# Attention block: four small moves around the key-tile loop, and the copy of the sums from ScalarE to VectorE

## Chip, cores, metric

One core of a Trainium2 chip. The metric is device time of one launch in microseconds; lower is better.

## The reference

```python
# x: 1 x 2048 x 640, H = 32 heads of Dh = 20
qkv = (layernorm(x) @ wqkv) -> q, k, v            # each 32 heads x 2048 x 20
p = softmax(einsum("bhqd,bhkd->bhqk", q, k) * 20 ** -0.5)
h = x + merge_heads(einsum("bhqk,bhkd->bhqd", p, v)) @ wo
out = h + (silu(layernorm(h) @ w_gate) * (layernorm(h) @ w_up)) @ w_down   # F = 1728
```

All tensors are float32.

## The kernel before

The program has three stages: the projections to q, k and v with layer norm (until about 320 us), the attention (until about 1445 us), and the feed-forward network. The change lies in the attention.

**Units.** Heads go in 8 groups of `G` = 4, queries in `NC` = 4 chunks of 512. A group g and a chunk c make a unit, u = 4 g + c, so there are `NU` = 32 units. Within a unit a loop runs over `NT` = 16 key tiles of 128 keys (`kt`). The instructions of each engine stand in the order in which Python writes them; nothing reorders them.

**One key tile.** The string `ORDER` = "WhSmsSHMs" gives the sequence of one key tile: W is the weighted sum of the values with the exponentials of two tiles ago (`weigh`, L1338, into the bank `acc`); S and s are the four score products (`scores`, L1328), each followed on ScalarE by an exponential (L1334, `probs`); h, H, m and M are products for later units' maxima (L272), whose results VectorE reduces (L292, L307) into `mx`. So a tile gives ScalarE four exponentials and VectorE three reductions. Each kind of product takes its banks in turn (`ps_one` four, `ps_max` three).

**Maxima.** Softmax needs each query's largest score before its exponentials. They are computed ahead, for the next one to two units. When a unit v has all of them (`full`), `max_all` reduces and negates them (L315, `neg`). They then go as extra rows into `queries[v]`, whose four rows the score products of unit v wait for:

- For units with c < 3, `max_parts` splits them on GpSimd, `max_turn` turns them on VectorE (L331) and stores them to DRAM (`m_d`, L332), and `max_load` loads them back (L342, four DMAs). The dictionary `later` says in which key tile each of these is issued, right behind W.
- For units with c = 3 (and unit 1), `max_finish` turns them on TensorE (L347), splits them on ScalarE and VectorE (L89, L90, `m`) and writes the rows with four DMAs (L354).

**End of a unit.** The last W of a unit runs in the second tile of the next unit's loop; right behind it `row_sums` copies `acc` to `o` (L1348) and sends the row sums to `r` (L1351, four DMAs). Later tiles of the same loop run `reciprocals` (L1359 on VectorE, its store L1361), `spread` (L1367, `rb`), a product on GpSimd (L1373), and the stores of the outputs (`store_o`, L1376, four DMAs to `o_d`).

**SyncE's queue.** All these DMAs, the loads of keys, values and queries for later units (L176, L193) and the stores and loads of weights that GpSimd prepares for the feed-forward network in between (`preparing`, L1137, L1166) go through SyncE's one queue in program order: one that waits holds those behind it.

Of the kernel before, what the change touches and what calls it, by code (L numbers as in the profile page):

```python
# [13 lines left out]
AF = mybir.ActivationFunctionType  # L14
# [16 lines left out]
NG = H // G  # L31
# [13 lines left out]
def tile_block(ctx: ExitStack, tc: tile.TileContext, x, wqkv, wo, wg, wu, wd, out):  # L45
    nc = tc.nc
# [41 lines left out]
    def split(src, hi, lo, lo_engine=nc.vector):  # L88
        nc.scalar.activation(hi, src, AF.Copy)  # L89
        lo_engine.tensor_tensor(out=lo, in0=src, in1=hi.bitcast(F32), op=ALU.subtract)  # L90
# [221 lines left out]
    def max_all(u):  # L312

        ends[u] = stk.tile([P, G * TPC], F32, name="neg", tag="neg", bufs=2)
        nc.vector.tensor_reduce(  # L315
            ends[u], mxs[u].rearrange("p b h t k -> p (b h t) k"), axis=AX.X, op=ALU.max, negate=True
        )
# [10 lines left out]
    def max_turn(u):  # L328

        turned = stk.tile([P, 2 * G * TPC], F32, name="turned", bufs=2)  # L330
        nc.vector.transpose(turned, ends.pop(u).bitcast(F32).rearrange("p i n -> p (i n)"))  # L331
        nc.sync.dma_start(m_d[u % 2], turned)  # L332

    def max_load(u):

        n = 2 * TPC
        rows = m_d[u % 2].rearrange("(q i r) c -> i r q c", q=4, i=2)
        for b in range(2):
            for i in range(2):
                row = b * ROW + NPART + i  # L340
                dst = queries[u][row : row + 1].bitcast(F32).rearrange("r j c -> r (j c)")
                nc.sync.dma_start(dst, rows[i, b * n : (b + 1) * n])  # L342

    def max_finish(u):

        m = (ps_one if u else ps_max)()[: G * TPC, :P]
        nc.tensor.transpose(m, ends.pop(u), ident)  # L347
        parts = stk.tile([G * TPC, 2, P], F32R, name="m2", tag="m2", bufs=1)
        split(m, parts[:, 0], parts[:, 1], nc.vector)
        for b in range(2):  # L350
            for i in range(2):
                row = b * ROW + NPART + i
                first = b * 2 * TPC
                nc.sync.dma_start(  # L354
                    queries[u][row : row + 1].bitcast(F32).rearrange(
                        "r j (t p) -> r (j t) p", t=TPC
                    ),
                    parts[first : first + 2 * TPC, i, :].bitcast(F32),
                )
# [963 lines left out]
    def scores(u, kt, j, probs):  # L1323

        p, b = divmod(j, 2)
        rows = slice(b * ROW, b * ROW + NPART + 2)
        ps = ps_one()
        nc.tensor.matmul(  # L1328
            ps,
            keys[u // NC][rows, p, kt * P : (kt + 1) * P],  # L1330
            queries[u][rows, p, :],
            start=True, stop=True,
        )
        nc.scalar.activation(probs[p][:, b, :], ps, AF.Exp, scale=scale)  # L1334
# [10 lines left out]

    def row_sums(acc, *queues):
        o = pc.tile([P, CH], F32, name="o", bufs=2)
        nc.scalar.activation(o, acc, AF.Copy)  # L1348
        r = pc.tile([P, 16], F32, name="r")
        for j in range(G):  # L1350
            queues[j % len(queues)].dma_start(  # L1351
                r[32 * j : 32 * j + 32, :],
                o[32 * j + DH : 32 * j + DH + 1, :].rearrange("r (p f) -> r p f", p=32),
            )
        return o, r
# [24 lines left out]
    todo, tail, accs, later, full, now = [], [], {}, {}, [], [0]  # L1380
    left = {u: sum(2 for a in rest if a[0] == u) for u in range(1, NU)}

    whole, halves_of = [], []

    def counted(u, n):
        left[u] -= n
# [3 lines left out]
    def next_max(b):  # L1390
        if not whole and rest:
            a = rest.pop(0)
            whole.extend((*a, i) for i in (b, 1 - b))
        if whole:
            a = whole.pop(0)
            max_one(*a)
            counted(a[0], 1)

    def next_half(b):

        if not halves_of and rest:
            a = rest.pop(0)
            halves_of.extend((i, a, []) for i in range(2))
        if not halves_of:
            return
        i, a, banks = halves_of[0]
        if not banks:
            banks.append(ps_max())
            max_half(banks[0], i, *a, b)
        else:  # L1410
            nc.tensor.keepalive_nop([nc.tensor.lower_ap(banks[0])])
            max_half(banks[0], i, *a, b)
            max_halves(banks[0], i, *a)
            counted(a[0], 2 * i)
            halves_of.pop(0)
# [11 lines left out]
    preparing = prepare_weights()  # L1427
# [3 lines left out]
    for u in range(NU):  # L1431
        g, c = divmod(u, NC)
        if g == NG - 1 and c >= 2:
            _, first, ln, flips, _ = ahead
            extra = [*first, *ln, lambda: None, *flips]
        for kt in range(NT):
            now[0] = u * NT + kt
            probs = [pp.tile([P, 2, CH], F32, name="probs") for _ in range(2)]
            heads = [[0, 2], [1, 3]]
            for op in ORDER if rest or whole or halves_of else LAST_ORDER:  # L1440
                if op in "mM":
                    next_max(int(op == "M"))
                elif op in "hH":
                    next_half(int(op == "H"))
                elif op in "sS":
                    scores(u, kt, heads[op == "S"].pop(0), probs)
                else:
                    if len(todo) == 2:
                        weigh_next()
                    for f in later.pop(now[0], ()):  # L1450
                        f()
                    if extra:
                        extra.pop(0)()
                    if preparing and u and kt not in (3, 4):
                        preparing.pop(0)()
                    if now[0] == (NU - NC) * NT + 8:
                        unit_ring, last_ring = weight_rings()
                        unit_ring.fill()
                        last_ring.fill()
            todo.append((u, kt, probs))  # L1460
            for v in full:
                max_all(v)
                if v % NC == NC - 1 or v == 1:
                    later.setdefault(now[0] + 2, []).append(lambda v=v: max_finish(v))
                else:
                    max_parts(v)
                    later.setdefault(now[0] + 4, []).append(lambda v=v: max_turn(v))
                    later.setdefault(now[0] + 6, []).append(lambda v=v: max_load(v))
            full.clear()
            if kt == 6 and u + 3 < NU:  # L1470
                load_queries(u + 3)
            if kt == 10 and u == 0:
                fill_ones(k_stk[1])
            if kt >= 8 and kt % 2 == 0 and c == 1 and g + 1 < NG:
                load_keys(g + 1, slice((kt - 8) // 2 * CH, (kt - 6) // 2 * CH))
            if kt >= 8 and kt % 2 == 0 and c == 2 and g + 1 < NG:
                load_values(g + 1, (kt - 8) // 2 * TPC, (kt - 6) // 2 * TPC)

            sooner = u >= NU - 2
            if kt == (3 if sooner else 4) and tail:  # L1480
                reciprocals(u - 1, tail[0][2], nc.sync)
                rb = spread(u - 1, nc.sync)
            if kt == (6 if sooner else 9) and tail:
                store_o(u - 1, tail[0][1], rb, nc.gpsimd, None)
            if kt == (7 if sooner else 11) and tail:
                store_o(u - 1, tail.pop()[1], rb, None, nc.sync)
            if g == NG - 1 and c >= 1:
                at = 8 if sooner else NT - 4
                if kt == at:
                    ahead = projection(  # L1490
                        c - 1, ps_max if c < NC - 1 else (lambda: ps_b())
                    )
                if kt in (at, at + 1, 12 if sooner else 14):
                    ahead[0][min(kt - at, 2)]()
                    if kt == at + 1 and c < NC - 1:
                        ahead[4]()
            k = 2 * (u - NU + 8)
            if kt in (12, 13) and 0 <= k + kt - 12 < ND:
                if k + kt == 12:
                    assert not preparing  # L1500
                    wo_hi = pc.tile([P, ND, D], F32R, name="wo_hi", bufs=1)
                    wo_lo = pc.tile([P, ND, D], F32R, name="wo_lo", bufs=1)
                load_wo(k + kt - 12)
            if kt in (2, 3) and 0 <= k + kt - 4 < ND:
                split_wo(k + kt - 4)
# [4 lines left out]
    u, o, r = tail.pop()  # L1510
# [561 lines left out]
```

## Time and profile before

| | us |
|---|---|
| median of 3 runs (lowest, highest) | 2011.97 (2009.52, 2014.36) |
| the profiled execution, and its span | 2012.87, 2010.4 |
| busy: TensorE, weight loads | 1985.1, 1268.7 |
| busy: VectorE, ScalarE, GpSimd | 1599.5, 1440.1, 789.4 |
| exponentials (L1334, 2048) | 1056.1 |
| reductions of maxima (L292 980, L307 492) | 671.8, 335.8 |

The granted TensorE clock was 0.999. A row of the timeline gives the start from the span's beginning, the duration, the engine, the line, the operation and the tile written and read; in brackets the engine's idle time ahead of it and what ended it. "q" behind an engine marks its queue (SPq: SyncE issuing a DMA). A row of the waits gives the waiter, who ended the wait, the total, the number and the longest.

### The profile page before, as it was taken

What the parts mean: (1) busy time and instruction counts of PE and PEld (TensorE: products, weight loads), DVE (VectorE), ACT (ScalarE), POOL (GpSimd) and SP (SyncE); (2) the same over time, 40 slices, a digit from 0 to 9 for tenths busy, and PEclk for the clock granted to TensorE, in tenths of its full rate; (3) what the DMA queues carried; (4) which work ended last, traced back from release to release, by engine and by line L of the source; (5) the groups of instructions that cost most, each with busy time, mean ns of one, the idle gap of its engine ahead of it and who ended that gap; (6) DMA issues with size and microseconds to landing.
All of it is one profiled execution on the core that took longest, in us unless ns stands there. A gap on an engine that the chain in (4) does not pass through costs nothing. (4 is left out here: it accounts for less than half of the span.)

```text
span 2010.4 us, 41923 instructions
## 1 busy us (share of the span) xinstructions
PE 1985.1 (99%) x14794; PEld 1268.7 (63%) x14794; DVE 1599.5 (80%) x2831; ACT 1440.1 (72%) x2827; POOL 789.4 (39%) x1182
## 2 busy tenths in 40 slices
PE   8999999999999999999999999999999999999998
PEld 6999995444444444444444444455598888888887
DVE  5687778899999899998999999975477666676667
ACT  4678778999999999999999999987633222212221
POOL 7464424343453443443400011011155544844465
PEclk9999999999999999999999999999999999999999
DMA  7887563443634544435412132222268655974642
GB/s 244 255 258 257 183 206 78 128 140 105 193 103 141 152 135 138 157 127 175 150 60 68 40 86 58 79 63 62 62 215 278 228 168 174 359 248 160 203 146 93
DMA packets 199350, 310.48 MB, mean 154 GB/s; under 512 B 53744, under 2 KB 87856, under 8 KB 198120
## 3 DMA queue, kind: packets, MB, share of 16 engines
q1 hardware_dynamic: 192552, 284.21, 44.0%
q0 software_dynamic: 6496, 23.60, 4.0%
q8 instruction: 120, 1.97, 0.4%
q14 instruction: 86, 0.70, 0.1%
q10 hardware_dynamic: 96, 0.00, 0.0%
HBM read 208.11 MB, written 99.19 MB: 153 GB/s over the span
## 5 line engine op out<-in xcount | busy, mean ns | idle before, releaser
L1334 ACT ACTIVATE probs<-ps_one 128x512 f32<-128x512 f32 x2048 | 1056.1, 612 | 46.7 <-PE ps_one L1328 37.2
L292 DVE TENSOR_REDUCE mx<-ps_max 128x1 f32<-128x512 f32 x980 | 671.8, 686 | 90.6 <-PE ps_max L272 88.0
L272 PEld LDWEIGHTS ps_max<-k_stk,q_stk 60*128 60x128 f32 x1964 | 294.2, 185 | 462.8 <-DVE mx L307 393.5
L1328 PE MATMUL ps_one<-q_stk,k_stk 62*128 62x512 f32 x2048 | 570.4, 427 | 2.7 <-DMA q_stk<-m 1.8
L272 PE MATMUL ps_max<-k_stk,q_stk 60*128 60x256 f32 (+1 forms) x1964 | 565.5, 376 | 2.5 <-DVE mx L292 1.2
L1338 PE MATMUL acc<-probs,v_stk 128*32 128x512 f32 x4096 | 546.1, 605 | 0.1
L307 DVE TENSOR_REDUCE mx<-ps_max 128x2 f32<-128x512 f32 x492 | 335.8, 683 | 0.4 <-PE ps_max L272 0.4
L1328 PEld LDWEIGHTS ps_one<-q_stk,k_stk 62*128 62x128 f32 x2048 | 304.9, 184 | 15.0 <-ACT probs L1334 11.3
L1750 DVE TENSOR_TENSOR tmp<-ps_a,tmp 128x512 f32<-128x512 f32 x208 | 141.3, 690 | 122.2 <-PE ps_a L1535 96.6
L262 DVE TENSOR_REDUCE mx<-ps_max 128x2 f32<-128x512 f32 x288 | 180.8, 685 | 63.7 <-PE ps_max L240 60.2
L252 ACT ACTIVATE ps_max<-ps_max 128x512 f32<-128x512 f32 x288 | 151.6, 583 | 42.9 <-PE ps_max L240 40.3
L1629 PE MATMUL ps_b<-halves,yp 128*128 128x320 f32 x1032 | 179.0, 308 | 1.5 <-DMA halves<-j_d 1.3
L1629 PEld LDWEIGHTS ps_b<-halves,yp 128*128 128x128 f32 x1032 | 165.2, 188 | 17.5 <-POOL yp L90 1.5
L1535 PE MATMUL ps_a<-t,units 128*128 128x512 f32 x624 | 162.5, 396 | 0.0
L1338 PEld LDWEIGHTS acc<-probs,v_stk 128*32 128x32 f32 x4096 | 80.7, 108 | 128.1 <-issue 119.9
L90 POOL TENSOR_TENSOR yp<-y,yp 128x256 fp32r<-128x256 f32 x96 | 60.2, 628 | 189.7 <-ACT yp L89 189.7
L1535 PE MATMUL ps_a<-z,units 128*128 128x512 f32 x516 | 133.8, 394 | 0.0
L1535 PEld LDWEIGHTS ps_a<-t,units 128*128 128x128 f32 x624 | 112.6, 188 | 18.5
L1373 POOL TENSOR_TENSOR o<-o,rb 128x512 f32<-128x512 f32 x31 | 39.8, 1284 | 194.2 <-DMA rb<-r_d 60.6
L1634 DVE TENSOR_TENSOR h<-ps_b,h 128x320 f32<-128x320 f32 x248 | 110.1, 482 | 6.8 <-PE ps_b L1629 5.4
L671 PE MATMUL ps_one<-z_hi,w_lo 64*128 64x512 f32 x380 | 113.4, 392 | 0.0
L671 PE MATMUL ps_one<-z_lo,w_hi 64*128 64x512 f32 x380 | 112.1, 392 | 0.0
(228 smaller groups left out, 2746.5 us busy)
## 6 DMA issues: line engine op xcount, KB each, us to landing
units<-w_d SPq DMA_DIRECT2D x186, 256.0 KB
w_d<-stage SPq DMA_DIRECT2D x106, 256.0 KB
halves<-j_d SPq DMA_DIRECT2D x70, 320.0 KB
j_d<-stage SPq DMA_DIRECT2D x42, 320.0 KB
k_stk<-k_d SPq DMA_DIRECT2D x64, 160.0 KB
q_stk<-q_d SPq DMA_DIRECT2D x64, 160.0 KB
raw<-k_d SPq DMA_DIRECT2D x62, 160.0 KB
raw<-q_d SPq DMA_DIRECT2D x54, 160.0 KB
```

What stands on the lines that cost most here:

```text
L252: nc.scalar.activation(ps, ps, AF.Relu)
L262: nc.vector.tensor_reduce(mx[:, b, :, t, kc], ps.rearrange("p (j n) -> p j n", j=2), axis=AX.X, op=ALU.max,)
L272: nc.tensor.matmul(ps, queries[u][rows, pair, t * P : (t + 1) * P], keys[u // NC][rows, pair, k0:k1], start=True, stop=True, skip_group_ch ...
L292: nc.vector.tensor_reduce(mx[:, b, pair, t, kc : kc + 1], ps, axis=AX.X, op=ALU.max)
L307: nc.vector.tensor_reduce(max_slots(u)[:, :, pair, t, slot], ps.rearrange("p (j n) -> p j n", j=2), axis=AX.X, op=ALU.max,)
L671: nc.tensor.matmul(ps, a[rows], b[rows], start=(i == n == 0), stop=(i == 1 and n == last), skip_group_check=True,)
L1328: nc.tensor.matmul(ps, keys[u // NC][rows, p, kt * P : (kt + 1) * P], queries[u][rows, p, :], start=True, stop=True,)
L1334: nc.scalar.activation(probs[p][:, b, :], ps, AF.Exp, scale=scale)
L1338: nc.tensor.matmul(acc[32 * j : 32 * j + 32, :], values[u // NC][:, kt, j * VW : j * VW + 32], probs[j // 2][:, j % 2, :], start=(kt == 0) ...
L1535: nc.tensor.matmul(ps.rearrange("p (t n) -> p t n", t=TPC), w[k][:, i], z[k][:, :, j], start=(first and m == 0), stop=(last and m == len(n ...
L1629: nc.tensor.matmul(ps, a, b, start=(n == 0), stop=(n == len(pairs) - 1))
L1750: add = lambda out, ps, x: nc.vector.tensor_tensor(out=out, in0=ps, in1=x, op=ALU.add)
```

## The change

1. `row_sums` copies `acc` on VectorE instead of ScalarE.
2. `max_turn` and `max_load` are issued 3 and 5 key tiles after `full` instead of 4 and 6. `max_finish` is issued at the end of the next tile's sequence instead of behind the W of the tile after that, through the new list `behind_step`; in a tile where that list holds something, no step of `preparing` is taken.
3. The keys of the next group are loaded in the first unit of a group instead of the second (except in group 0).
4. The reciprocals come at tile 5 instead of 4, except in the last two units.
5. In units with c = 2 (except unit 30) the four output stores come at tile 13 instead of 11.

```diff
     def row_sums(acc, *queues):
         o = pc.tile([P, CH], F32, name="o", bufs=2)
-        nc.scalar.activation(o, acc, AF.Copy)
+        nc.vector.tensor_copy(o, acc)
...
-                    if preparing and u and kt not in (3, 4):
+                    if preparing and u and kt not in (3, 4) and not behind_step:
                         preparing.pop(0)()
...
             todo.append((u, kt, probs))
+            while behind_step:
+                behind_step.pop(0)()
             for v in full:
                 max_all(v)
                 if v % NC == NC - 1 or v == 1:
-                    later.setdefault(now[0] + 2, []).append(lambda v=v: max_finish(v))
+                    behind_step.append(lambda v=v: max_finish(v))
                 else:
                     max_parts(v)
-                    later.setdefault(now[0] + 4, []).append(lambda v=v: max_turn(v))
-                    later.setdefault(now[0] + 6, []).append(lambda v=v: max_load(v))
+                    later.setdefault(now[0] + 3, []).append(lambda v=v: max_turn(v))
+                    later.setdefault(now[0] + 5, []).append(lambda v=v: max_load(v))
...
-            if kt >= 8 and kt % 2 == 0 and c == 1 and g + 1 < NG:
+            if kt >= 8 and kt % 2 == 0 and c == (0 if g else 1) and g + 1 < NG:
                 load_keys(g + 1, slice((kt - 8) // 2 * CH, (kt - 6) // 2 * CH))
...
-            if kt == (3 if sooner else 4) and tail:
+            if kt == (3 if sooner else 5) and tail:
                 reciprocals(u - 1, tail[0][2], nc.sync)
                 rb = spread(u - 1, nc.sync)
             if kt == (6 if sooner else 9) and tail:
                 store_o(u - 1, tail[0][1], rb, nc.gpsimd, None)
-            if kt == (7 if sooner else 11) and tail:
+            if kt == (7 if sooner else 13 if c == 2 else 11) and tail:
                 store_o(u - 1, tail.pop()[1], rb, None, nc.sync)
```

VectorE's order at the start of unit 11, after the change. `mx_134` holds maxima of a later unit; L292 and L307 are the three reductions of a key tile.

```order
L292 TENSOR_REDUCE mx_134<-ps_max 128x1 x2
L307 TENSOR_REDUCE mx_134<-ps_max 128x2
L292 TENSOR_REDUCE mx_134<-ps_max 128x1
L1348 COPY o<-acc 128x512
L292 TENSOR_REDUCE mx_134<-ps_max 128x1
L307 TENSOR_REDUCE mx_134<-ps_max 128x2
L292 TENSOR_REDUCE mx_134<-ps_max 128x1 x2
```

Before, nothing stood between these two L292; the copy is new on this engine, between the last reduction of one tile and the first of the next.

VectorE's order some key tiles later in unit 11, before the change:

```order
L307 TENSOR_REDUCE mx_134<-ps_max 128x2
L292 TENSOR_REDUCE mx_134<-ps_max 128x1
L1359 RECIPROCAL r<-r 128x16
L292 TENSOR_REDUCE mx_135<-ps_max 128x1
L307 TENSOR_REDUCE mx_134<-ps_max 128x2
L292 TENSOR_REDUCE mx_135<-ps_max 128x1
L315 TENSOR_REDUCE neg<-mx_134 128x16
L292 TENSOR_REDUCE mx_135<-ps_max 128x1
```

and after it:

```order
L292 TENSOR_REDUCE mx_134<-ps_max 128x1
L292 TENSOR_REDUCE mx_135<-ps_max 128x1
L307 TENSOR_REDUCE mx_134<-ps_max 128x2
L292 TENSOR_REDUCE mx_135<-ps_max 128x1
L315 TENSOR_REDUCE neg<-mx_134 128x16
L1359 RECIPROCAL r<-r 128x16
L292 TENSOR_REDUCE mx_135<-ps_max 128x1
```

The reciprocal has moved one tile on and now stands directly behind L315.

SyncE's queue in the second half of unit 10 (c = 2), before the change. `v_stk` are values for the next group, `w_d` prepared weights, `q_stk<-m` the four rows of maxima for unit 11.

```order
L193 DMA v_stk_5606<-v_d 128x4x96 x2
L1376 DMA o_d<-o 20x512 x4
L1137 DMA w_d_86<-stage 128x512
L193 DMA v_stk_5606<-v_d 128x4x96
L354 DMA q_stk<-m_11431 1x8x128 x4
```

and after it:

```order
L193 DMA v_stk_5606<-v_d 128x4x96 x2
L354 DMA q_stk<-m_11412 1x8x128 x4
L193 DMA v_stk_5606<-v_d 128x4x96
L1376 DMA o_d<-o 20x512 x4
L193 DMA v_stk_5606<-v_d 128x4x96
```

The rows of maxima have passed the output stores, one value load and the weight store; the output stores now come behind them.

More of the change, by code (lines that the diff above doesn't have):

```diff
@@ L1381, in tile_block @@
     left = {u: sum(2 for a in rest if a[0] == u) for u in range(1, NU)}
-    whole, halves_of = [], []
+    whole, halves_of, behind_step = [], [], []
     def counted(u, n):
```

## The prediction

> **What bounds the kernel now.** I read the page first, then the windows of the attention, the waits of ScalarE and VectorE in it, and last the timeline around the starts of units. The page alone misleads:
>
> ```profile
> PE 1985.1 (99%) x14794; PEld 1268.7 (63%) x14794; DVE 1599.5 (80%) x2831; ACT 1440.1 (72%) x2827; POOL 789.4 (39%) x1182
> POOL 7464424343453443443400011011155544844465
> ```
> ```profile
> 500.00:600.00 100.00, 100.00 (x766) 42.54 (x765) 91.70 (x157) 99.43 (x195) 45.74 (x85) 1.00 0.48 148
> ```
> ```profile
> ACT probs L1334 <- PE ps_max L272: 4.5, 5, 1.5
> ...
> DVE r L1359 <- DMA r<-o: 2.6, 2, 1.6
> ```
>
> In a quiet stretch of the attention (second fence: TensorE, weight loads, VectorE, ScalarE, GpSimd) TensorE shows 100, ScalarE 99.4 and VectorE 91.7 of 100 us. One of the first two sets the pace; which one is read from the timeline, here around the start of unit 13 and then of unit 11:
>
> ```profile
> 760.78 1.07 PE L1338 MATMUL acc<-probs,v_stk 128*32 128x512 f32 x8
> ...
> 762.84 1.06 PE L1338 MATMUL acc<-probs,v_stk 128*32 128x512 f32 x8
> 763.04 0.68 DVE L307 TENSOR_REDUCE mx<-ps_max 128x2 f32<-128x512 f32 x1
> 763.63 0.68 DVE L292 TENSOR_REDUCE mx<-ps_max 128x1 f32<-128x512 f32 x1
> 763.84 0.38 PE L272 MATMUL ps_max<-k_stk,q_stk 60*128 60x256 f32 x1
> ...
> 764.24 0.63 ACT L1348 ACTIVATE o<-acc 128x512 f32<-128x512 f32 x1
> ...
> 764.49 0.69 DVE L292 TENSOR_REDUCE mx<-ps_max 128x1 f32<-128x512 f32 x1 [0.17 <-PE ps_max L272]
> ...
> 764.92 1.06 PE L1338 MATMUL acc<-probs,v_stk 128*32 128x512 f32 x8
> ...
> 765.91 0.38 PE L272 MATMUL ps_max<-k_stk,q_stk 60*128 60x256 f32 x1
> ...
> 767.30 1.06 PE L1338 MATMUL acc<-probs,v_stk 128*32 128x512 f32 x8
> ```
> ```profile
> 695.46 2.07 ACT L1334 ACTIVATE probs<-ps_one 128x512 f32<-128x512 f32 x4 [1.54 <-PE ps_max L272]
> 697.38 0.63 ACT L1348 ACTIVATE o<-acc 128x512 f32<-128x512 f32 x1
> ```
>
> One key tile is one L1338 group to the next: 762.84 - 760.78 = 2.06, call it 2.07 us. After a wait ScalarE starts four exponentials and then the copy in 697.38 - 695.46 = 1.92 us. So ScalarE could do a tile in 1.92 and has 0.15 to spare; its 99% is only pace taken from TensorE, which goes from the weighted sums to the next maximum product without a hole (762.84 + 1.06 against 763.84). TensorE's order of products is the bound. Time is lost where it waits: at the copy in each unit, twice at a reciprocal, and at five unit starts.
>
> **The copy of the sums.** Now: the tile with the copy lasts 767.30 - 764.92 = 2.38, that is 0.31 too long. ScalarE explains it: 1.92 + 0.48 for the copy = 2.40. The change puts the copy into VectorE's queue, behind a tile's last maximum and ahead of the next tile's first.
>
> ```profile
> L1348 ACT ACTIVATE o<-acc 128x512 f32<-128x512 f32 x32 | 20.1, 628 | 1.0 <-PE acc L1338 1.0
> ```
> ```profile
> L758 DVE COPY e<-ps_one 128x512 f32<-128x512 f32 x1 | 0.7, 692 | 0.7 <-issue 0.7
> ```
>
> The nearest row for VectorE's price is the one PSUM copy of this shape that it does (692 ns), as long as a maximum, and maxima start 0.60 apart (763.04, 763.63). Then: last maximum 763.63, copy 764.23 (the sums are done by then, 762.84 + 1.06), next maximum 764.83 instead of 764.49, the following L307 at 765.43, its end 766.11. The product at 765.91 needs that bank; the signal takes 0.05 (671.60 + 0.68 to 672.33, rows below), so it starts at 766.16, 0.25 late. What is queued behind the copy are three maxima; TensorE waits for the second. So each copy still costs 0.25 instead of 0.31. The scheme holds in units 1 to 29: 29 x 0.06 = 1.7 us won. The ends: if the copy took its whole 0.69 on VectorE, 0.34 is lost and the term is -0.9; if VectorE hid it all, 29 x 0.31 = +9.0. I stay at 1.7, since the 0.60 spacing is measured for the same shape and bank type. In the two last units and at the end maxima are few and VectorE idles; there I charge 0.06 once for the longer copy, 0.1.
>
> [...]
>
> **Reciprocals one key tile later (units 1 to 29).**
>
> ```profile
> 669.94 1.07 PE L1338 MATMUL acc<-probs,v_stk 128*32 128x512 f32 x8
> ...
> 673.35 1.06 PE L1338 MATMUL acc<-probs,v_stk 128*32 128x512 f32 x8
> ```
> ```profile
> 670.89 0.25 DVE L1359 RECIPROCAL r<-r 128x16 f32<-128x16 f32 x1 [1.55 <-DMA r<-o]
> 671.06 0.63 DVE L292 TENSOR_REDUCE mx<-ps_max 128x1 f32<-128x512 f32 x1
> 671.60 0.68 DVE L307 TENSOR_REDUCE mx<-ps_max 128x2 f32<-128x512 f32 x1
> ```
> ```profile
> 672.33 0.50 PE L272 MATMUL ps_max<-k_stk,q_stk 60*128 60x512 f32 x1
> ```
>
> In unit 10 VectorE stood 1.55 us at the reciprocal, whose sums came late by DMA; TensorE lost 673.35 - 669.94 - 2.07 = 1.34. The other of the two waits is 2.6 - 1.55 = 1.05, less the 0.17 that VectorE idles in a tile anyway (764.49): 0.88. A tile later (2.07) both sums are there: in unit 10 the reciprocal would stand at 670.89 - 1.55 + 2.07 = 671.41, 0.5 after they came. Won: 2.2; 0.9 if unit 10 still waits. The two DMAs behind it (r_d, rb) move too, past nothing; SyncE's queue is held a tile later, and behind it stand the query loads for three units on, which nobody awaits. GpSimd's product keeps four tiles, 8.3 us.
>
> In the odd units (15 of 29) the reciprocal now lands behind the small reduction L315:
>
> ```profile
> 909.59 0.24 DVE L315 TENSOR_REDUCE neg<-mx 128x16 f32<-128x96 f32 x1
> 909.90 0.69 DVE L292 TENSOR_REDUCE mx<-ps_max 128x1 f32<-128x512 f32 x1
> ```
>
> Such small ones start 0.17 to 0.20 apart (670.89, 671.06): the maximum comes at 909.97 instead of 909.90. The bank is free 0.07 early (763.72 + 0.05 against 763.84), so it costs nothing. At full lengths it is 0.17 - 0.07 = 0.10, 15 times, 1.5 lost.
>
> **Maxima sooner, keys a unit sooner, some output stores later: the unit starts.** Five starts hold ScalarE 4.5 us together (the waits above), 1.54 at unit 11. The scores wait for rows of maxima that come by SyncE's queue:
>
> ```profile
> 648.31 0.35 SPq L332 DMA_DIRECT2D m_d<-turned  x1
> 648.71 3.46 SPq L176 DMA_DIRECT2D k_stk<-k_d  x4
> 653.99 2.79 SPq L342 DMA_DIRECT2D q_stk<-m_d  x4
> ```
> ```profile
> 687.39 1.42 SPq L1376 DMA_DIRECT2D o_d<-o  x4
> ...
> 690.85 2.82 SPq L354 DMA_DIRECT2D q_stk<-m  x4
> ```
> ```profile
> 687.48 0.28 DVE L90 TENSOR_TENSOR m<-ps_one,m 16x128 fp32r<-16x128 f32 x1 [0.21 <-ACT m L89]
> ```
> ```profile
> 684.58 0.73 POOL L1178 TENSOR_TENSOR sums<-raw 128x256 f32<-128x256 f32 x1 [20.96 <-DMA raw<-in_B_w_up]
> ...
> 686.09 1.28 POOL L1373 TENSOR_TENSOR o<-o,rb 128x512 f32<-128x512 f32 x1
> ```
>
> In unit 9 the store m_d and the loads of it stand between key loads; the change takes these (16 per group, 96 in all) to the unit before and asks for the maxima 2.07 sooner. That ends two of the waits. In unit 10 the parts of m are ready at 687.76, but their loads start at 690.85, behind output stores that waited for GpSimd's product until 687.39, a weight store and a value load. With the 4 stores of seven such units behind them, the loads can start some 3 us sooner, against 1.54 of waiting. Yet a weight store that waits for GpSimd can still stand ahead, so I take 3.9 of 4.5; 1.5 if the three waits behind the output stores stay. Turning sooner costs VectorE nothing new: one operation per unit in the same idle 0.17.
>
> **The last unit's maxima of a group** (L347 now ahead of the weighted sums):
>
> ```profile
> 685.82 1.06 PE L1338 MATMUL acc<-probs,v_stk 128*32 128x512 f32 x8
> 686.81 0.28 PE L347 MATMUL ps_one<-ident,neg 128*16 128x128 f32 x1
> 688.24 1.07 PE L1338 MATMUL acc<-probs,v_stk 128*32 128x512 f32 x8
> ```
>
> This tile takes 2.42, 0.35 too much. Ahead of the sums, ScalarE's split comes sooner, but the transpose must wait for a score bank sooner too. I take no change for seven units; ends +2.5 (7 x 0.35) and -2.0 (7 x 0.28 on top). The skipped step of weight preparation moves GpSimd by a tile in these units; its zeros from slice 20 on cover that.
>
> **Sum.** 1.7 - 0.1 + 2.2 + 0 + 3.9 + 0 = 7.7 us. The profiled execution took 2012.87 (span 2010.4), 0.9 above the median 2011.97: 2005.2 from the one, 2004.3 from the other. Forecast 2004.7, its own range 2001 to 2008.
>
> **Rivals.**
> 1. *ScalarE is the bound.* [...] Worked out in rows: each copy would free its 0.48 whole, 29 x 0.48 = 13.9, with 2.2 and 3.9 that is 20.0 and 1992.4. For it stands 99.4%; against it 1.92 per tile and the 0.31 loss, not 0.48. Chance 0.04.
> 2. *The wait changes its name.* SyncE is still held by weight stores that wait for GpSimd (20.96 above), the three waits stay, and the copy gains nothing: 2.2 + 1.5 = 3.7, 2008.7. For it: GpSimd's holes are untouched. Chance 0.23.
> 3. *Slower: late sums.* The key loads now end just before the second unit of a group, where the reciprocal's sums (r<-o) queue behind them, as they did in unit 10 (issued at 664.88, row below). VectorE then stands at the reciprocal in six units. It costs from 0.5 us later than in unit 10 on, and outweighs the rest from 0.5 + 7.7 / 6 = 1.8 later; at 2.9 later each of the six units costs 2.4, together 14.4 - 7.7 = 6.7 more than now: 2018.7. Against it: in the first unit of a group no loads of maxima share the last eight tiles with the keys, so the queue should be shorter than it was. Chance 0.07.
>
> ```profile
> 664.88 2.76 SPq L1351 DMA_DIRECT2D r<-o  x4
> ```
>
> **Chances.** Forecast 0.66, rivals 0.04, 0.23, 0.07. About 0.2% (4.0 us) can be told from no change: faster by more than that 0.70, within it 0.22 (rival 2 mostly), slower 0.08. The range takes in rival 2 and the better end of the copy in part: 1999.5 to 2010.
>
> **Right or wrong.** In the changed trace: right if the L1338 tile after the copy is 2.32 long, if no DVE r L1359 wait on r<-o is left, if ScalarE's waits on ps_max are under 1 us, and if the L342 and L354 loads end 2 us before a unit. Wrong if that tile is 2.07 or 2.41, if r<-o waits come up in units 5, 9, 13, or if L347's tile differs from 2.42 by more than 0.1.

## The result, and the profile after

| | before | after | ratio (95% interval) |
|---|---|---|---|
| median of 7 runs each, us | 2011.97 (2009.52 to 2014.36) | 2005.26 (2002.82 to 2009.37) | 0.9968 (0.9958 to 0.9978) |
| the profiled execution, and its span | 2012.87, 2010.4 | 2007.38, 2005.6 | |
| a later set on one chip, 9 and 5 runs | 2011.70 | 2001.82 | 0.9955 (0.9943 to 0.9968) |

So the changed kernel is faster by 0.2 to 0.6%, where 0.36% was forecast. The page after the change, in the same columns as before:

```profile
PE 1980.9 (99%) x14794; PEld 1261.1 (63%) x14794; DVE 1616.8 (81%) x2863; ACT 1430.2 (71%) x2795; POOL 790.2 (39%) x1182
```

VectorE has taken 32 operations and some 17 us of work, and the time fell all the same. ScalarE has lost 10 us of work, and the time fell by 6.7. The page alone does not tell the bound; the run of the copy alone, below, tells more. The waits of the attention after the change (waiter, who ended the wait, total us, number, longest):

```profile
DVE r L1359 <- DMA r<-o: 1.2, 1, 1.2
DVE turned L331 <- POOL neg L324: 0.3, 1, 0.3
```

ScalarE's wait on ps_max, 4.5 us in five pieces before, is no longer listed: all five unit starts run through. One wait for r is left, and one is new. The timeline around the copy of unit 13, the same place as before:

```profile
759.47 1.07 PE L1338 MATMUL acc<-probs,v_stk 128*32 128x512 f32 x8
...
760.25 0.68 DVE L292 TENSOR_REDUCE mx<-ps_max 128x1 f32<-128x512 f32 x1
760.85 0.68 DVE L1348 COPY o<-acc 128x512 f32<-128x512 f32 x1
761.45 0.68 DVE L292 TENSOR_REDUCE mx<-ps_max 128x1 f32<-128x512 f32 x1
761.59 1.07 PE L1338 MATMUL acc<-probs,v_stk 128*32 128x512 f32 x8
762.05 0.68 DVE L307 TENSOR_REDUCE mx<-ps_max 128x2 f32<-128x512 f32 x1
762.59 0.38 PE L272 MATMUL ps_max<-k_stk,q_stk 60*128 60x256 f32 x1
762.65 1.36 DVE L292 TENSOR_REDUCE mx<-ps_max 128x1 f32<-128x512 f32 x2
763.16 0.72 PE L272 MATMUL ps_max<-k_stk,q_stk 60*128 60x256 f32 x2
763.81 1.06 PE L1338 MATMUL acc<-probs,v_stk 128*32 128x512 f32 x8
765.88 1.06 PE L1338 MATMUL acc<-probs,v_stk 128*32 128x512 f32 x8
```

From weighted sum to weighted sum: 2.12, then 2.22, then 2.07 again. The first tile loses 0.05, because the sums at 761.59 cannot begin until the copy has left `acc` (760.85 + 0.68 = 761.53). The second loses 0.15. The half product at 762.59 is on time, 1.00 behind the weighted sum as in the tile before; what is late is the last maximum product of the tile, the second of the two in the x2 row. It starts together with the last score product, which has a row of its own in the timeline of TensorE alone:

```profile
763.39 0.49 PE L1328 MATMUL ps_one<-q_stk,k_stk 62*128 62x512 f32 x1
```

That is 0.05 behind the end of the first of the two reductions (762.65 + 0.68 = 763.33), which frees a bank. So a copy costs 0.20 now, against 0.31 before.

### The profile page after: what moved, and what is told of

It reads as the page before. It is cut to its first block, busy times and chain, and to the rows that moved or that the text cites. A ratio compares the mean times of both kernels' runs of the same rounds, so it can differ in the third digit from the quotient of the medians.

```text
span 2005.6 us, 41837 instructions
## 1 busy us (share of the span) xinstructions
PE 1980.9 (99%) x14794; PEld 1261.1 (63%) x14794; DVE 1616.8 (81%) x2863; ACT 1430.2 (71%) x2795; POOL 790.2 (39%) x1182
## 5 line engine op out<-in xcount | busy, mean ns | idle before, releaser
L292 DVE TENSOR_REDUCE mx<-ps_max 128x1 f32<-128x512 f32 x980 | 671.2, 685 | 71.2 <-PE ps_max L272 68.3
L1328 PE MATMUL ps_one<-q_stk,k_stk 62*128 62x512 f32 x2048 | 564.2, 425 | 0.9 <-DVE m L90 0.9
L307 DVE TENSOR_REDUCE mx<-ps_max 128x2 f32<-128x512 f32 x492 | 335.8, 682 | 0.4 <-PE ps_max L272 0.4
```

The lines of the kernel that those rows point to most:

```text
L292: nc.vector.tensor_reduce(mx[:, b, pair, t, kc : kc + 1], ps, axis=AX.X, op=ALU.max)
L307: nc.vector.tensor_reduce(max_slots(u)[:, :, pair, t, slot], ps.rearrange("p (j n) -> p j n", j=2), axis=AX.X, op=ALU.max,)
L1328: nc.tensor.matmul(ps, keys[u // NC][rows, p, kt * P : (kt + 1) * P], queries[u][rows, p, :], start=True, stop=True,)
```

## How the runs are read

All runs below are compared with the kernel before, run on the same chip in the same session. Besides the ratio I use the three waits above, totalled over the attention, since each is tied to one place. "none" means that the wait is not listed.

| kernel | ratio (95% interval) | ScalarE on ps_max | VectorE on r | VectorE on GpSimd's parts |
|---|---|---|---|---|
| before | 1 | 4.5 | 2.6 | none |
| after | 0.9968 (0.9958, 0.9978) | none | 1.2 | 0.3 |
| after, second time | 0.9955 (0.9943, 0.9968) | none | none | none |
| copy alone | 0.9995 (0.9986, 1.0003) | 6.4 | 2.3 | none |
| keys alone | 0.9984 (0.9974, 0.9993) | 2.3 | none | none |
| all but the copy | 0.9976 (0.9967, 0.9985) | none | none | 0.4 |
| all but the keys | 0.9962 (0.9950, 0.9975) | 0.4 | 2.5 | 0.5 |
| all but the output stores | 0.9964 (0.9950, 0.9978) | 0.6 | none | 1.0 |
| all but the reciprocals | 0.9962 (0.9949, 0.9975) | none | none | none |
| all but max_finish's place | 0.9995 (0.9985, 1.0005) | 5.9 | 0.3 | none |
| that, with the step left out | 0.9963 (0.9950, 0.9975) | none | 0.6 | none |

The two rows of the same program set the measure: waits of 1.2 and 0.3 us are there in one execution and not in the other. A wait of about one us in one profile is no proof of an edit's effect.

## The experiments

**The copy alone.** The kernel before with one line changed.

```diff
-        nc.scalar.activation(o, acc, AF.Copy)
+        nc.vector.tensor_copy(o, acc)
```

> The kernel before with one edit: the copy of the sums on VectorE. My theory (TensorE's order is the bound): the loss per copy in units 1 to 29 falls from 0.31 to 0.20 us, as in the changed kernel's trace, so about 3.3 us less, 2008.7; all five waits at unit starts (4.5 us) and the waits at the reciprocals (2.6 us) stay. Rival 1 (ScalarE is the bound): 29 x 0.48 = 13.9 us less, 1998. Rival (the copy gains nothing on VectorE): 2012.

Measured: 2012.02 us against 2013.3, no gain that can be told from nothing. The tiles at the copies did become shorter: over units 1 to 29 the time beyond 2.069 in the two tiles around the copy fell from 8.6 to 6.1 us. Of the 6.1, 1.5 lie in unit 19 alone, where the granted clock was 0.51 from 966.6 to 970.0 us; without that unit it fell from 8.3 to 4.6. But the unit starts, the tile ahead of these, rose from 5.1 to 7.1, which takes most of the 2.5 back:

```profile
ACT probs L1334 <- PE ps_max L272: 6.4, 5, 1.9
```

ScalarE's 4.5 became 6.4: the starts of units 10 and 19 each wait 0.9 longer, the other three as before, within 0.1. The rows of maxima come when SyncE, the DMAs and GpSimd have them ready, and units that get there sooner may only wait longer; then the terms of the prediction's sum are not independent. Two longer waits in one profile do not show that this is so. In this profile the undisturbed tile was some 5 ns longer too, for which see the last section. The run also speaks against ScalarE as the bound: it was freed of all 32 copies, 20.1 us, and by the interval at most 2.8 us came of it.

**All but the copy.** The changed kernel with that line put back.

```diff
-        nc.vector.tensor_copy(o, acc)
+        nc.scalar.activation(o, acc, AF.Copy)
```

> The changed kernel with the copy back on ScalarE. My theory: the L1338 tile after the copy is 2.38 long again, 29 x 0.11 = 3.3 us slower than the changed kernel, 2008.6, and the waits at unit starts stay away. If the copy and the waits are tied together, waits of ScalarE on ps_max come back too and it is 5 us or more slower; if the copy is worth nothing, 2005.

Measured: 2008.32, ratio 0.9976, near the 2008.6 expected. Two other kernels of the same session, each with the copy on VectorE and one other part undone, came at 0.9962 and 0.9964, so the copy is worth 2 to 3 us once the starts no longer wait; the intervals overlap, and the trace carries it: 8.6 us at the copies again, and no wait at a start. With that the copy's 0.31 against 0.20, 29 times, 3.2 us, is what it brings when nothing behind it waits.

**The keys, put back and alone.** In the changed kernel the loads return to the second unit of a group; in the other kernel they are all that is changed.

```diff
-            if kt >= 8 and kt % 2 == 0 and c == (0 if g else 1) and g + 1 < NG:
+            if kt >= 8 and kt % 2 == 0 and c == 1 and g + 1 < NG:
```

> The changed kernel with the keys loaded in the second unit of a group again. My theory: the starts of units 10 and 18 wait for the rows of maxima again, 0.4 and 1.0 us, less whatever the sooner turn saves; with 2.07 us sooner I expect the first to stay away and 0 to 0.5 at unit 18. The reciprocal of unit 10 comes a tile later, so its wait stays away. Together 0 to 1 us slower than the changed kernel, 2005.3 to 2006.3. Rival: the keys are what freed unit 11 too (through the late sums, queries and weights of unit 10): up to 3 us slower, 2008.

> The kernel before with one edit: keys a unit sooner. My theory after the last runs: the key loads are what made the sums, GpSimd's product and the rows of maxima late, so four or five of the waits at unit starts (4.5 us) go, and the wait at unit 10's reciprocal (1.3 us) too: 4.5 to 5.8 us less than before, 2006 to 2007.5. Rival: each of the waits needs its own edit (stores, sooner turn), and the keys alone give the two at units 10 and 18: 1.5 us less, 2010.5.

Measured with the keys put back: 2006.47, 0.9962. The waits of this kernel:

```profile
ACT probs L1334 <- PE ps_max L272: 0.4, 1, 0.4
DVE r L1359 <- DMA r<-o: 2.5, 2, 1.3
DVE turned L331 <- POOL neg L324: 0.5, 1, 0.5
```

The waits for r are back, in units 2 and 14, although the reciprocals stood a tile later. Of the two starts that the keys were said to hold, unit 10 waits again, 0.42 (before: 0.44), and unit 18 does not (before: 1.02). I had expected it the other way round, and why it came so is open. With the keys alone: 2007.88, 0.9984, an interval wholly below 1; the 3.2 us lie between my expectation and its rival. Both waits for r are gone, with the reciprocals at their old tile 4, and of the five waits at starts those of units 10 and 18:

```profile
ACT probs L1334 <- PE ps_max L272: 2.3, 3, 1.3
```

What is left are units 11, 15 and 19. So the moved keys, not the moved reciprocals, ended the wait for r in unit 10: its sums are sent (L1351) 4.1 us after the first weighted sums of the unit's loop here, 8.1 in the kernel before, 7.4 with the keys put back. The wait in unit 2 the keys cannot have ended: this kernel differs from that before only from unit 4 on. In the medians the loss of the keys in the full change did not show.

**All but the output stores, all but the reciprocals.**

```diff
-            if kt == (7 if sooner else 13 if c == 2 else 11) and tail:
+            if kt == (7 if sooner else 11) and tail:
```

> The changed kernel with all output stores at tile 11. My theory: in units with c = 2 the stores wait for GpSimd's product ahead of the loads of the maxima, so waits come back at the starts of units 11, 15, 19: up to 1.5 + 0.5 + 0.9 = 2.9 us slower, 2008.2. Rival: with the keys gone from the unit before, GpSimd's product is no longer late, the stores hold nothing, and it stays at 2005.3.

```diff
-            if kt == (3 if sooner else 5) and tail:
+            if kt == (3 if sooner else 4) and tail:
```

> The changed kernel with the reciprocals at tile 4 again. My theory: the late reciprocals were bought against sums that come late in the units whose key loads end just before; those are now units 2, 5, 9, 13, 17, 21 and 25. At tile 4 a wait of 2 to 3 us at unit 2 (1.2 there now) and up to 1 us in one or two of the others; 2 to 4 us slower than the changed kernel, 2008. Rival: with the keys moved no sums are late any more apart from unit 2, so only that wait grows by 2.07: 2007.

Measured: 2005.47 (0.9964) and 2003.37 (0.9962). With the output stores put back, one of the three starts that they were said to hold waits again, unit 19, by 0.6 us:

```profile
ACT probs L1334 <- PE ps_max L272: 0.6, 1, 0.6
DVE turned L331 <- POOL neg L324: 1.0, 1, 1.0
```

With the reciprocals put back no wait is left at all. The loss that I had expected came in neither. With the rest of the change in place neither edit is needed for what it gained, and neither does harm that can be measured.

**All but max_finish's place.** The changed kernel, with `max_finish` again behind the W of the tile after next; then `behind_step` is always empty and no step of the weight preparation is left out.

```diff
-                    behind_step.append(lambda v=v: max_finish(v))
+                    later.setdefault(now[0] + 2, []).append(lambda v=v: max_finish(v))
```

> The changed kernel with the transpose of the last unit's maxima (L347) behind the weighted sums of the tile after, as before. My theory: that tile stays 0.35 too long in seven units, so nothing changes there; the steps of weight preparation come a tile sooner from unit 3 on, which shifts SyncE's queue and may move the wait at unit 2's reciprocal by up to 1 us either way: 2004.3 to 2006.3. Rival: the new place hides part of the transpose and undoing it costs 1 to 2 us, 2007.

Measured: 2009.65, 0.9995. No gain is left that can be told from none (at most 3 us by the interval), by an edit that I had put at nothing. SyncE's queue in unit 10, GpSimd and ScalarE of this kernel:

```profile
673.83 0.43 SPq L1166 DMA_DIRECT2D raw<-in_B_w_gate  x1
674.31 0.66 SPq L1166 DMA_DIRECT2D raw<-in_B_w_up  x1
675.08 1.70 SPq L176 DMA_DIRECT2D q_stk<-q_d  x4
679.13 0.93 SPq L193 DMA_DIRECT2D v_stk<-v_d  x2
688.16 0.34 SPq L1137 DMA_DIRECT2D w_d<-stage  x1
688.55 0.43 SPq L193 DMA_DIRECT2D v_stk<-v_d  x1
689.08 2.83 SPq L354 DMA_DIRECT2D q_stk<-m  x4
```
```profile
682.80 0.73 POOL L1178 TENSOR_TENSOR sums<-raw 128x256 f32<-128x256 f32 x1 [17.19 <-DMA raw<-in_B_w_up]
...
687.39 0.74 POOL L1147 TENSOR_TENSOR stage<-raw,stage 128x256 fp32r<-128x256 f32 x1
```
```profile
693.70 2.61 ACT L1334 ACTIVATE probs<-ps_one 128x512 f32<-128x512 f32 x5 [2.01 <-PE ps_max L272]
```

Between the value load that ended at 680.06 and the weight store at 688.16 SyncE issued nothing for 8 us: the store waited for the piece that GpSimd finished at 687.39 + 0.74 = 688.13, and GpSimd had itself stood 17 us for a weight load. The four rows of maxima stood behind it, and unit 11 waited 2.01. The same place in the changed kernel:

```profile
680.88 2.05 SPq L193 DMA_DIRECT2D v_stk<-v_d  x2
685.77 2.83 SPq L354 DMA_DIRECT2D q_stk<-m  x4
688.64 0.44 SPq L193 DMA_DIRECT2D v_stk<-v_d  x1
689.18 1.50 SPq L1376 DMA_DIRECT2D o_d<-o  x4
```

There is no weight store ahead of the rows, and they go out 3.3 us sooner. But the edit did two things: it moved the transpose on TensorE by half a tile, and it left out steps of the weight preparation, whose stores and loads go through SyncE's queue. The next run parts them.

**The old place, with the step left out.** As above, but the step of weight preparation in the tile ahead of `max_finish` is not taken.

```diff
+                    held.add(now[0] + 1)
...
-                    if preparing and u and kt not in (3, 4) and not behind_step:
+                    if preparing and u and kt not in (3, 4) and now[0] not in held:
```

> The changed kernel, with max_finish back behind the W of the tile after next (its old place on TensorE and ScalarE), but the step of weight preparation in the tile ahead of it still left out, so that no weight store stands ahead of the four L354 loads in SyncE's queue in unit 10; a value load of 0.9 us still does. Theory (the order in SyncE's queue is what freed the starts of units 11, 15 and 19): the L354 issue starts at about 687 us instead of 689.1 (old place, no step left out) or 685.8 (changed kernel); ScalarE's waits on ps_max are under 1.2 us together instead of 5.9, the starts cost TensorE under 0.8 us instead of 5.8, and the median ratio to the kernel before is 0.996 to 0.9975. Rival (it is the place on TensorE and ScalarE, half a tile sooner, that counts): the waits stay at 4 to 6 us and the ratio at 0.999 to 1.0005. In both the L347 tile is 2.40 to 2.42.

Measured: 2004.38, 0.9963, and no wait on ps_max; its interval does not meet that of the run without the skip, and both have the transpose at the same time of the same tile:

```profile
683.56 1.07 PE L1338 MATMUL acc<-probs,v_stk 128*32 128x512 f32 x8
684.56 0.28 PE L347 MATMUL ps_one<-ident,neg 128*16 128x128 f32 x1
685.99 1.06 PE L1338 MATMUL acc<-probs,v_stk 128*32 128x512 f32 x8
```
```profile
673.81 1.60 SPq L176 DMA_DIRECT2D q_stk<-q_d  x4
...
679.00 0.39 SPq L1166 DMA_DIRECT2D raw<-in_B_w_gate  x1
679.49 0.47 SPq L1166 DMA_DIRECT2D raw<-in_B_w_up  x1
680.31 3.04 SPq L193 DMA_DIRECT2D v_stk<-v_d  x3
685.22 2.82 SPq L354 DMA_DIRECT2D q_stk<-m  x4
688.14 1.52 SPq L1376 DMA_DIRECT2D o_d<-o  x4
...
690.19 0.92 SPq L1137 DMA_DIRECT2D w_d<-stage  x2
```

The rows go out at 685.22 instead of 689.08, sooner than the 687 expected, and the weight stores stand behind. So it is shown: what freed the starts of units 11, 15 and 19 is that steps of the preparation are left out, through the order in SyncE's queue. It is not the one step in the tile ahead of the rows, though. `preparing` is worked off one step a tile, so each step left out puts all later ones a tile back, and by unit 10 that had happened in units 2 and 6. Without the skip the weight loads (L1166) stand ahead of the query loads of tile 6 (675.08, first fence); here they come behind them, two tiles later by the program, and so do the pieces made from them and their stores. The step that unit 10 itself puts off is, by the list in `prepare_weights`, the second pair of sums (L1182, L1183), which issues no DMA. This last part is read from the program and the two queues; no run leaves out a single step.

The place on TensorE is worth nothing at these starts; if anything the old one is better, by the end of the attention: unit 30 lasts 53.92 to 53.98 us in the five profiles with the old place and 54.42 to 54.49 in the nine with the new one.

**Three attempts at a better version.** First the last score product ahead of the last maximum product in the tile that showed the 0.15 (`SWAPPED` = "WhSmsSHsM" for key tile 2); then that with the reciprocals at tile 4; then that with the maxima turned and loaded at 4 and 6 again. In the last session the changed kernel itself ran beside them.

```diff
-            for op in ORDER if rest or whole or halves_of else LAST_ORDER:
+            for op in (SWAPPED if kt == 2 else ORDER) if rest or whole or halves_of else LAST_ORDER:
```

> The changed kernel with the last two products of tile 2 of each unit swapped (s ahead of M). My theory: of the 0.20 us that a copy still costs, 0.15 arises at M of tile 2, whose bank VectorE frees late (M starts at 0.05 behind its place and the score product behind it waits too); with s ahead, 0.05 to 0.10 of it goes, 1.5 to 2.9 us in 29 units: 2003. Rival: the time is lost at the bank as such, the next weighted sums wait for M as before, and nothing changes: 2005.3; slower by up to 1 us if the pairing of M and s on TensorE suffers.

> The changed kernel with the reciprocals back at tile 4 and the fourth exponential's product ahead of the second maximum product in tile 2 of each unit. Theory (each saves its own piece: the wait of VectorE for r in unit 2, 1.2 us, and what the earlier run of the swap showed): attention stage from unit 1 to 29 at 936 to 937.5 us instead of 939.0, no wait on r<-o, median 1.5 to 2.5 us under the changed kernel's, ratio 0.995 to 0.9965 to the kernel before. Rival (what those runs gained was a difference between profiles of the steady tile, a few ns per tile): within 0.7 us of the changed kernel on the same chip.

> As the run with swap and reciprocals, and the turning and loading of the maxima back at 4 and 6 tiles behind full. Theory (sooner was not needed once the keys were moved, and it made VectorE wait for GpSimd's parts in unit 8): no wait of turned<-neg (0.3 to 1.0 us in the runs with the sooner turn), no new wait at a unit's start, 0.3 to 1.0 us less than with the sooner turn. Rival (the loads were needed sooner too): waits of ScalarE on ps_max of 1 us or more at the starts of units 10 or 18, and the time the same or up to 1 us more.

> The changed kernel itself, on the chip of the three others, so that they can be compared with it and not only with the kernel before: ratio 0.9958 to 0.9978 as before. Theory: its steady key tile is again 2.076 us against 2.069 of the kernel before, if the few nanoseconds belong to the program; the rival, that they vary from one loading to the next, gives 2.069 in this profile or 2.076 in some of the kernels with ScalarE's copy.

Measured: the swap 2003.84 (0.9960; 0.9946 to 0.9975), with the reciprocals 2004.0 (0.9961; 0.9949 to 0.9974), with the turn put back 2004.42 (0.9961; 0.9947 to 0.9975); the changed kernel beside the last two 2001.82. The expectation of a gain failed: none beats it. The swap left the copies at 5.3 us over 29 units, as in the changed kernel, so the bank, not the product's place, holds that tile. With the turn back at its old tile the wait on GpSimd's parts was not there, but in the second run of the changed kernel neither was it.

## Why the prediction held, and where it did not

The forecast, 2004.7, lies 0.6 us under the median of the seven runs and 2.9 over that of the later five; both medians are in the range. The terms, by the two profiled executions:

| term | forecast, won | found, won | from |
|---|---|---|---|
| copy | 1.7 | 3.3 | time beyond 2.069 in the two tiles around it, units 1 to 29: 8.6 to 5.3 |
| end of the attention | -0.1 | -0.5 | unit 30: 53.98 to 54.42 |
| reciprocals | 2.2 | 1.3 (2.2 in the second execution) | TensorE's tiles at the waits for r: 2.2 to 1.0 |
| unit starts | 3.9 | 4.4 | the same, in the tile ahead of these: 5.1 to 0.7 |
| the transpose, L347 | 0 | 0 | its tiles' time beyond 2.07, seven units: 2.5 before and after |
| turning sooner | 0 | -0.3 (0 in the second) | the new wait on GpSimd's parts |
| sum | 7.7 | 8.2 | |

That the sum comes so near is in part luck: the copy won more than was forecast, the reciprocals and the end of the attention less, and the starts were freed by something else than the sum had it.

**Right.** TensorE's order of products is the bound and ScalarE is not; rival 1, 13.9 us for the copies, is excluded by the copy alone. The collision of the reciprocal with L315 cost nothing that shows. The new place of the copy gave a tile between the two that would have refuted it: 2.22, not 2.07 or 2.41. Of the four signs named for being right two came: no wait on ps_max is left, and the loads of the rows are all issued at least 3.4 us before the unit's first exponential. The tile of 2.32 did not come, and one wait for r is left in the first execution.

**The copy was mis-sized.** Of its step, 0.60 from the start of a maximum to that of the copy and 0.60 on to the next maximum were right (760.25, 760.85, 761.45). Wrong was who waits for that: the half product, said to be 0.25 late because of L307's bank, is on time, and the 0.20 comes from `acc` (0.05) and from the bank behind a later L292 (0.15). So 0.11 is won per copy instead of 0.06. The group of the copies, with count, total and mean of one:

```profile
L1348 DVE COPY o<-acc 128x512 f32<-128x512 f32 x32 | 21.8, 682 | 1.0 <-PE acc L1338 0.7 <-issue 0.3
```

The forecast took the length of one from a row of before, 692 ns; in the changed kernel it is 682. What counts in the queue is shorter: the next operation started 0.60 after the copy did (760.85, 761.45).

**The reciprocals: right in sum, wrong in cause.** The step "a tile later both sums are there" fell in its own terms: in the profile of the changed kernel unit 2 still waits.

```profile
396.20 3.47 SPq L1351 DMA_DIRECT2D r<-o  x4
...
402.95 0.25 DVE L1359 RECIPROCAL r<-r 128x16 f32<-128x16 f32 x1 [1.18 <-DMA r<-o]
```

Before, these sums had been sent at 393.54:

```profile
393.54 3.89 SPq L1351 DMA_DIRECT2D r<-o  x4
```

The reciprocal went one tile on, and its data came 2.7 us later. That is not chance: in the eight profiles with the reciprocals at tile 5 the sums of unit 2 are sent 7.1 to 8.5 us after the first weighted sums of the unit's loop, in the six with tile 4 after 4.2 to 6.0. VectorE waits for them in four of the eight and in one of the six. What in the queue delays them was not followed up. Unit 10's wait went because of the keys, as they remove it alone; and leaving the reciprocals where they were costs nothing. Rival 3, that the moved keys would delay the sums in units 5, 9 and 13, was too small to cost anything: in the changed kernel those of unit 13 are sent after 5.4 us instead of 4.1, and nothing waits. With the keys put back it is unit 14 that waits, 1.2 us.

**The unit starts: right in size, wrong in the edit that did it.** The sum gave the starts of units 11, 15 and 19 to the output stores; with the rest in place they are worth 0.6 us at one of them. The weight store that the prediction named as a risk was the obstacle that counted, and rival 2's mechanism was real: without the skipped steps the three starts wait 5.9 us and the time cannot be told from that of before. It did not come about only because of the edit that I booked under "the last unit's maxima of a group", where I counted its transpose and put the skipped step down to GpSimd's idle time. That is the step that failed: I took the skip for a tile of GpSimd's time, and did not ask where it leaves the weight stores in SyncE's queue, although the rows of the queue showed the maxima passing one. That the shifted stores fell behind the rows, and not ahead of them, was luck.

**The transpose and the turn.** L347's place was put at nothing:

```profile
682.04 1.06 PE L1338 MATMUL acc<-probs,v_stk 128*32 128x512 f32 x8
684.22 0.28 PE L347 MATMUL ps_one<-ident,neg 128*16 128x128 f32 x1
684.43 1.06 PE L1338 MATMUL acc<-probs,v_stk 128*32 128x512 f32 x8
686.53 1.07 PE L1338 MATMUL acc<-probs,v_stk 128*32 128x512 f32 x8
```

2.39 and 2.10: the 0.35 is now spread over two tiles and unchanged in sum, as forecast. What the new place does cost lies in unit 30, the 0.5 us at the end of the attention, which the sum did not have; the moved copy alone leaves that unit at 53.92. "Turning sooner costs VectorE nothing new" was not quite so: asked for a tile sooner, GpSimd's parts were not always there, 0.3 to 1.0 us in unit 8, in five of the ten profiles with the sooner turn.

## What to carry to other kernels

Price every step that is moved or left out by all that it issues, and read the queue it issues into in program order: here one weight store, waiting for an idle-looking engine, stood ahead of four small loads, and its place decided whether a gain could be seen at all. In a list that is worked off one step a tile, a step left out shifts everything behind it, so read the queue in later units too. Terms of a sum that end in waits on something with its own pace need not be independent (indicated here, not shown): make the late data come sooner first. And before a wait of one us in one profile is explained, look at a second profile of the same program.

## What had not been expected of the hardware

The steady key tile has two lengths, a few ns apart, in one and the same program. Ten undisturbed tiles of the changed kernel in its first profile:

```profile
906.09 1.07 PE L1338 MATMUL acc<-probs,v_stk 128*32 128x512 f32 x8
...
926.85 1.06 PE L1338 MATMUL acc<-probs,v_stk 128*32 128x512 f32 x8
```

and in its second:

```profile
902.54 1.06 PE L1338 MATMUL acc<-probs,v_stk 128*32 128x512 f32 x8
...
923.21 1.06 PE L1338 MATMUL acc<-probs,v_stk 128*32 128x512 f32 x8
```

2.076 against 2.067, at a granted clock of 1.00 in both stretches (0.998 and 1.000 over the whole spans). Over the 380 or so undisturbed tiles of each the means are 2.0734 and 2.0679, together 2.1 us; the kernel before has 2.0690. Of the four kernels run on that one chip in the last session two had the short tile and two the long one, so neither the chip nor one of the edits sets it; what does is open. The feed-forward network, which no edit touches, also took from 568.4 us (before) to 570.1 (after) and 571.8 (all but the copy); in the last of these the granted clock was 0.50 there for 3.4 us, from 1469.9 on. That is why the spans of the two first profiles are only 4.8 us apart where the places named above add up to 8.2, and why medians and waits, not stage lengths of two profiles, carry the argument here.
